# A spectral and gated-FFN kernel: new order and cut of the loads and of the first matmuls

## The chip, the core and the metric

The kernel runs on one core of one Trainium2 chip. The core has five engines that run beside each other: TensorE (PE, with its weight loads shown as PEld), VectorE (DVE), ScalarE (ACT), GpSimd (POOL) and SyncE (SP). [...] Matmuls write to PSUM; everything else lives in SBUF, and transfers from and to the device's memory (HBM) are issued by SP, ACT or POOL and carried by 16 DMA engines. The metric is the device time of one execution in microseconds. The page and the views quoted here come from one profiled execution.

## The reference

The input `x` has 2048 rows of 640 values. What is computed:

```python
xn = layernorm(x)                                  # over the 640 values of a row
X  = rfft2(xn) * (w_r + 1j * w_i)                  # over rows and columns, weights 2048 x 321
s  = irfft2(X, s=(2048, 640)).astype(bfloat16)
g  = silu((gelu(xn @ w_gate) * (xn @ w_up)) @ w_down)   # 640 -> 1536 -> 640
return x + s * g
```

All inputs are bf16. `B_x` is not used.

## The kernel before

**Tiling.** The 2048 rows are taken as 16 slabs of 128 rows (`n1` from 0 to 15; slab `n1` holds the rows n1, n1 + 16, and so on), which all live in the tile X. Four slabs make a group `g` of 512 rows. The FFN's inner width of 1536 is 12 tiles `t` of 128. Wg and Wu hold the gate and up weights as 5 row blocks (`c`, 128 rows each of the 640) by 1536 columns; Wd holds the down weights.

**Stages.** The two transforms are matrix products with cosine and sine tables that the kernel makes itself on POOL, DVE and ACT (Tinv, Tfwd, FT, FI, MG). The forward part works slab by slab (`slab_S1`, `slab_D`), goes through a scratch tensor ZDR in HBM, is read back as the tile B, multiplied by the weights W1 and W2 in eleven bursts (`s2_step`, tiles px, xs, pu), goes through a second scratch tensor UDR, and is transformed back (`slab_S1i`, `slab_Di`, `group_*`, `finish`). The FFN goes group by group: first the 12 tiles of gate and up products, then the down products, which for groups 1 and 2 are made with fewer multiplications from sums (`product`, `u_sum`, `w_sum`).

**The order of the work.** It is written out by hand. The list `back` holds the FFN's pieces in the order of PE, and `plan[s]` holds what is issued right after piece `s`; `put(s, ...)` adds to it. Every engine gets its instructions in that order and never changes it. The second stage starts at piece `sb`.

**The opening.** SP loads slab 0 (`load_x(0, 1)`) and slab 1, then up weights and the next slabs in turn; ACT loads the gate weights of tiles 0 to 5, two tiles at a time (`load_w(0, t, t + 2, nc.scalar)`). Each load of two tiles reads rows of 256 columns, 512 bytes. A load takes one of eight semaphores in turn, and so waits until the eighth load before it has landed. DVE makes the statistics of a slab in two halves (`bn_half`, line 189) and joins them (`bn_join`, line 195); the reciprocal root comes from ACT for slab 0 (`root_act`, line 214, which then also loads the table for Gelu) and from POOL for the others (`root`: `ve` on DVE, line 205, then a power on POOL, line 207). `norm_parts` normalises a slab in two parts, columns 0 to 383 and 384 to 639 (line 218). `slab_Tparts` transposes the slab on PE against the identity (line 994, tile pt) and copies the parts to the transposed tile xnT, in XG, the first on DVE and the second on ACT (line 995). While PE has nothing to do it runs fillers on a tile of ones (`warm_pe`, line 588, tile GEN): 21 at the start and 2 after the first transposes.

The order on DVE at the start is: statistics of slab 0, first half of slab 1, second half of slab 1, its join, its `ve`, and then the norm of slab 0:

```python
1136    warm_pe(21)
1137    bn_half(1, 1)
1138    bn_join(1)
1139    root(1, 1)
1140    norm_parts(0)
1141    slab_Tparts(0)
1142    warm_pe(2)
```

**The first pieces.** `ffn_piece(g, t, k, c0, c1_)` makes one tile `t` of gate (k = 0) or up (k = 1) for the columns c0 to c1_ of xnT: five matmuls, one for each row block, into a half or a quarter of a PSUM bank (psg or psu, two buffers each), and then the eviction: Gelu on ACT for the gate (line 837, tile ge), the product with ge on DVE for the up (line 839, tile UT). Group 0 starts with tiles 0 and 1 for slab 0 alone (128 columns), then for slab 1, then tiles 2 to 7 for slabs 0 and 1 (256 columns), then tiles 0 to 7 for slabs 2 and 3. These are 18 gate and 18 up pieces, each with an eviction of its own. From tile 8 on the pieces have all 512 columns.

Of the kernel before, what the change touches and what calls it, by code (L numbers as in the profile page):

```python
# [76 lines left out]
def build(nc, env):  # L77
    consts, big, wts, work, psA, psB = (env[k] for k in ("consts", "big", "wts", "work", "psA", "psB"))
    ZDR, UDR, X, Wg, Wu, Wd, W1, W2 = (env[k] for k in ("ZDR", "UDR", "X", "Wg", "Wu", "Wd", "W1", "W2"))
    xv, outv, wgv, wuv = (env[k] for k in ("xv", "outv", "wgv", "wuv"))  # L80
    A_w_r, A_w_i, B_w_down = (env[k] for k in ("A_w_r", "A_w_i", "B_w_down"))

    def load_x(n0, n, eng=nc.sync):
        eng.dma_start(out=X[:, n0:n0 + n, :], in_=xv[:, n0:n0 + n, :])

    def load_w(k, t0, t1, eng=nc.sync):
        f0, f1 = t0 * P, t1 * P
        eng.dma_start(out=(Wg, Wu)[k][:, :, f0:f1], in_=(wgv, wuv)[k][:, :, f0:f1])
# [12 lines left out]
    load_gu(6, 8)  # L101
    load_x(4, 4)
    load_gu(8, 12)
    load_x(8, 4)
    nc.sync.dma_start(out=Wd, in_=B_w_down.rearrange("(t p) d -> p t d", p=P))
    load_x(12, 4)

    spw = [(WT, src.rearrange("(k1 r) l -> k1 r l", k1=NS)) for WT, src in ((W1, A_w_r), (W2, A_w_i))]

# [63 lines left out]
    def c1(name, dt=FP32):  # L173
        return consts.tile([P, 1], dt, name=name)
# [11 lines left out]
    def bn_half(n1, k):  # L186
        if k == 0:
            st_n[n1] = work.tile([P, 2, nc.vector.BN_STATS_DIM], FP32, tag="st", bufs=3, name="st")
        nc.vector.bn_stats(out=st_n[n1][:, k, :], in_=X[:, n1, 320 * k:320 * k + 320])  # L189

    def bn_join(n1):
        g = n1 // 4
        if g not in mva:
            mva[g] = work.tile([P, 4, nc.vector.BN_AGGR_DIM], FP32, tag="mva", bufs=2, name=f"mva{g}")
        nc.vector.bn_aggr(out=mva[g][:, n1 % 4, :], in_=st_n[n1])

    def stats(n1):
        for k in range(2):
            bn_half(n1, k)
        bn_join(n1)  # L200

    def root(n0, n):
        m = mva[n0 // 4][:, n0 % 4:n0 % 4 + n, :]
        ve = work.tile([P, 4], FP32, tag="ve", name="ve")[:, 0:n]
        nc.vector.tensor_scalar(out=ve, in0=m[:, :, 1], scalar1=1e-5, scalar2=None, op0=ALU.add)  # L205
        r = work.tile([P, 4], FP32, tag="rst", bufs=4, name="rst")[:, 0:n]
        nc.gpsimd.tensor_tensor(out=r, in0=ve, in1=mhalf[:, 0:n], op=ALU.pow)  # L207
        rall[n0] = r
        for k in range(n):
            rstd[n0 + k] = r[:, k:k + 1]  # L210

    def root_act(n1):
        rstd[n1] = c1("rst0")
        nc.scalar.activation(out=rstd[n1], in_=mva[n1 // 4][:, n1 % 4, 1:2], func=ACT.Abs_reciprocal_sqrt, bias=eps)
        nc.scalar.activation(out=warm, in_=negpi, func=ACT.Gelu_apprx_tanh)

    def norm(n1, c0=0, c1_=D):
# [10 lines left out]
    eps = c1("eps")  # L228
    nc.vector.memset(eps, 1e-5)
# [95 lines left out]

    fwd_consts()
    vt_iota(0)
    stats(0)
    bn_half(1, 0)
    root_act(0)  # L330

# [252 lines left out]
    def warm_pe(n):  # L584
        if not warm_bank:
            warm_bank.append(bank(0))
        for _ in range(n):
            nc.tensor.matmul(warm_bank[0][:, 0:256], lhsT=ones[:, 0:P], rhs=ones, start=True, stop=True)
# [230 lines left out]
    def bank(k):  # L819
        return psA.tile([P, 512], FP32, tag="gu"[k], name="ps" + "gu"[k])  # L820
# [5 lines left out]
    def ffn_piece(g, t, k, c0, c1_):  # L826
        for j in range(c0 // P, c1_ // P):
            assert ("T", 4 * g + j) in done
        ps = bank(k)[:, c0:c1_]
        WT = (Wg, Wu)[k]  # L830
        for c in range(5):
            nc.tensor.matmul(ps, lhsT=WT[:, c, t * P:(t + 1) * P], rhs=xnT[g][:, c, c0:c1_],  # L832
                             start=(c == 0), stop=(c == 4))
# [7 lines left out]
    def ffn_part(g, t, h):  # L841
        for k in range(2):
            ffn_piece(g, t, k, h * 256, h * 256 + 256)

    def ffn_half(g, t, k):
        ffn_piece(g, t, k, 0, 512)
# [8 lines left out]
    def flush():  # L855
        now = put_off[:]
        del put_off[:]
        for f in now:
            f()
# [109 lines left out]
            if t == NT - 1:  # L969
                gated(g, j, k, ph)  # L970

    def ffn_slab(j, tk):
        for t, k in tk:
            ffn_piece(0, t, k, j * P, j * P + P)

    GG, UU = ((0, 0), (1, 0)), ((0, 1), (1, 1))

    def run(*items):
        for it in items:
            it[0](*it[1:])  # L980

    PARTS = ((0, 3), (3, 5))

    def norm_parts(n1):
        for a, b in PARTS:
            norm(n1, a * P, b * P)

    def slab_Tparts(n1):
        if n1 == 0:
            xnT[0] = slot(0, 5, 512)  # L990
        for (a, b), ev in zip(PARTS, (nc.vector.tensor_copy, nc.scalar.copy)):
            pt = psB.tile([P, 5, P], BF16, tag="b")
            for c in range(a, b):
                nc.tensor.transpose(out=pt[:, c, :], in_=X[:, n1, c * P:(c + 1) * P], identity=ident)  # L994
# [5 lines left out]
    back = [(run, (ffn_slab, 0, GG), (norm_parts, 1), (slab_Tparts, 1), (vt_iota, 1), (ffn_slab, 0, UU),  # L1000
             (inv_consts, 0), (inv_consts, 1)),
            (run, (ffn_slab, 1, GG + UU), (stats, 2), (root, 2, 1))]
    for h in range(2):
        for t in range(0 if h else 2, NP):
            back.append((ffn_part, 0, t, h))
        if h == 0:
            back[-1] = (run, (ffn_piece, 0, NP - 1, 0, 0, 256), (slab_Tparts, 3), (ffn_piece, 0, NP - 1, 1, 0, 256))
    for g in range(4):
        for t in range(NP if g == 0 else 0, NT):
            for k in range(2):  # L1010
# [10 lines left out]
    def put(s, *item):  # L1021
        plan[s].append(item)

    put(1, inv_rest)
    put(2, norm, 2)
    put(3, bn_half, 3, 0)
    put(4, bn_half, 3, 1)
    put(4, bn_join, 3)
    put(4, root, 3, 1)
    put(4, slab_T, 2, 1)  # L1030
    put(5, norm, 3)
    for g in range(5):
        put(3 + g, ft_v, g)
        put(8 + g, ft_v, 5 + g)
# [110 lines left out]

# [35 lines left out]
```

## Time and profile before

| | us |
|---|---|
| Median of 3 runs | 193.76 (193.47 to 193.83) |
| Profiled execution, its own time | 193.65 |
| Span in the profile, first to last instruction | 191.9 |
| PE busy | 186.1 (97%) |
| DVE busy | 150.9 (79%) |
| ACT busy | 131.9 (69%) |
| POOL busy | 53.9 (28%) |

The page gives the busy time of each engine, the chain of work that ended last, and groups of equal instructions. The chain is followed back from the last instruction: at each step to what released it, or to the instruction before it on its engine. The timeline lists instructions in order of time: start, duration, engine, line, operation, what it writes and reads, and in brackets the idle time of its engine just before and what ended it. A row that stands for several instructions has their count (x5). "SPq" and "ACTq" are the queues from which loads are issued. Matmul durations include the pipeline's length, so that they overlap; the distance between starts says what each costs.

### The profile page before, as it was taken

Reading aid. Unit: us, or ns where it says so; the run is one execution under the profiler, and the core shown is the slowest. Engines: PE = TensorE matmul, PEld = TensorE weight load, DVE = VectorE, ACT = ScalarE, POOL = GpSimd, SP = SyncE. Lnnn points to the kernel's source line nnn. Section 1 sums busy time; section 2 is a strip of 40 time slices with the busy share of each in tenths; the row PEclk is TensorE's granted clock in tenths of the full one; section 3 lists DMA queues with packets and bytes.
Section 4 is the critical chain, followed back from the end, with each engine's and each line's share of the span. In section 5 each row is a group of like instructions: output and inputs, shape, how many; then the busy total and the mean of one; then the engine's idle time right before and its main releaser. Section 6 shows DMA issues by size and latency. Waiting matters only on the chain.

```text
span 191.9 us, 4068 instructions
## 1 busy us (share of the span) xinstructions
PE 186.1 (97%) x1453; PEld 115.6 (60%) x1469; DVE 150.9 (79%) x364; ACT 131.9 (69%) x241; POOL 53.9 (28%) x91
## 2 busy tenths in 40 slices
PE   7999999999999999999999999999999999999993
PEld 5788854677655665566543334347775555556772
DVE  6787889899799889846978677685445898888973
ACT  4658557957878778536697878634989776876622
POOL 4458768999040200000000000002030134150400
PEclk9999999999999999999999999999999999999999
DMA  6999999948889994249996444149900084778842
GB/s 164 300 329 360 370 332 170 172 99 318 178 165 191 211 300 120 78 111 230 223 108 123 106 103 103 42 107 273 266 5 0 0 117 111 152 153 213 121 174 62
DMA packets 39700, 32.43 MB, mean 169 GB/s; under 512 B 12928, under 2 KB 37760, under 8 KB 39552
## 3 DMA queue, kind: packets, MB, share of 16 engines
q1 hardware_dynamic: 35888, 27.91, 58.6%
q0 software_dynamic: 1824, 3.28, 9.4%
q10 hardware_dynamic: 1968, 0.98, 1.9%
q8 instruction: 11, 0.18, 0.4%
q14 instruction: 9, 0.07, 0.1%
HBM read 19.03 MB, written 7.88 MB: 140 GB/s over the span
## 4 chain that ended last, share of the span: by engine, by line
PE 95%; DMA 2%; DVE 1%; issue 1%; SPq 0%; ACT 0%
PE psu L832 27%; PE psg L832 27%; PE psg L967 7%; PE psg L933 7%; PE psu L967 6%; PE psu L933 5%; PE pu L657 2%; PE pd L762 2%; PE pv L735 2%; PE pz L555 2%; PE pd L573 2%; PE px L628 2%; DMA X<-in_A_x_dram 2%; PE pt L994 1%; PE pd L575 1%
## 5 line engine op out<-in xcount | busy, mean ns | idle before, releaser
L832 PE MATMUL psu<-XG,Wu 128*128 128x512 bf16 (+2 forms) x284 | 60.4, 342 | 0.5 <-issue 0.3
L832 PE MATMUL psg<-XG,Wg 128*128 128x512 bf16 (+2 forms) x280 | 60.1, 341 | 0.6
L839 DVE TENSOR_TENSOR UT<-psu,ge 128x512 bf16<-128x512 f32 (+2 forms) x58 | 34.4, 594 | 13.6 <-PE psu L832 8.1
L837 ACT ACTIVATE ge<-psg 128x512 bf16<-128x512 f32 (+2 forms) x58 | 30.3, 523 | 21.3 <-PE psg L832 20.6
L832 PEld LDWEIGHTS <-Wu 128*128 128x128 bf16 x290 | 25.9, 98 | 20.9 <-issue 3.4
L832 PEld LDWEIGHTS <-Wg 128*128 128x128 bf16 x290 | 26.5, 98 | 18.8 <-issue 0.2
L967 PEld LDWEIGHTS <-UT 128*128 128x128 bf16 x204 | 19.1, 98 | 6.9
L813 POOL DMA_DIRECT2D VY<-in_A_x_dram x12 | 10.6, 964 | 26.2 <-ACT W L737 10.5
L713 POOL COPY vr<-VY 128x128 bf16<-128x128 bf16 x2 | 0.6, 291 | 60.2 <-DMA VY<-UDR 60.2
L644 DVE TENSOR_TENSOR RZ<-xs,W 128x960 bf16<-128x960 bf16 (+2 forms) x22 | 13.3, 647 | 4.4 <-ACT xs L640 4.4
L967 PE MATMUL psg<-Wd,UT 128*128 128x320 bf16 (+1 forms) x108 | 15.7, 290 | 0.0
L578 ACT CAST RZ<-pd 128x660 bf16<-128x660 f32 x16 | 11.3, 706 | 5.2 <-PE pd L575 5.2
L189 DVE BATCH_NORM_STATS2 st<-X 128x6 f32<-128x320 bf16 x32 | 14.0, 476 | 0.6 <-DMA X<-in_A_x_dram 0.4
L933 PEld LDWEIGHTS <-UT 128*128 128x128 bf16 x120 | 11.4, 98 | 4.8 <-issue 0.4
L967 PE MATMUL psu<-Wd,UT 128*128 128x320 bf16 (+1 forms) x96 | 13.9, 293 | 0.0
L737 ACT CAST W<-pv 128x640 bf16<-128x640 f32 x16 | 11.1, 691 | 3.1 <-PE pv L735 3.1
L763 ACT ACTIVATE W<-pd 128x640 bf16<-128x640 f32 x16 | 11.3, 706 | 1.5 <-PE pd L762 1.5
L557 ACT CAST GEN<-pz 128x640 bf16<-128x640 f32 x16 | 11.2, 698 | 1.2 <-PE pz L555 1.2
L672 ACT CAST RX<-pu 128x480 bf16<-128x480 f32 (+3 forms) x22 | 10.8, 489 | 1.1 <-DVE RX L672 0.3
L640 ACT CAST xs<-px 128x960 bf16<-128x960 f32 (+2 forms) x11 | 10.3, 933 | 0.0
L207 POOL TENSOR_TENSOR rst<-ve,mhalf 128x1 f32<-128x1 f32 (+1 forms) x6 | 5.5, 913 | 11.5 <-DVE ve L205 11.5
L933 PE MATMUL psg<-X,UT 128*128 128x320 bf16 x48 | 7.8, 300 | 0.0
(202 smaller groups left out, 302.1 us busy)
## 6 DMA issues: line engine op xcount, KB each, us to landing
ZDR<-RZ SPq DMA_DIRECT2D x16, 160.5 KB, 4.1
UDR<-RX SPq DMA_DIRECT2D x10, 240.8 KB, 3.1
B<-ZDR SPq DMA_DIRECT2D x8, 240.8 KB, 5.2
W<-UDR SPq DMA_DIRECT2D x2, 963.0 KB, 9.1
X<-in_A_x_dram SPq DMA_DIRECT2D x3, 640.0 KB, 10.3
Wd<-in_B_w_down_dram SPq DMA_DIRECT2D x1, 1920.0 KB, 14.6
VY<-in_A_x_dram POOLq DMA_DIRECT2D x12, 160.0 KB, 4.3
out_dram<-VY SPq DMA_DIRECT2D x12, 160.0 KB, 2.8
```

The lines of the kernel that those rows point to most:

```text
L189: nc.vector.bn_stats(out=st_n[n1][:, k, :], in_=X[:, n1, 320 * k:320 * k + 320])
L557: nc.scalar.copy(out=Zt[n1], in_=pz)
L578: nc.scalar.copy(out=zd.rearrange("p c (q e) -> p c q e", e=10), in_=pd[:, :, 0:330].rearrange("p c (e q) -> p c q e", q=33))
L644: nc.vector.tensor_tensor(out=pp[-1], in0=xs, in1=WT[:, :, h0:h0 + n, l0:l0 + w], op=ALU.mult)
L672: copy(out=out, in_=src)
L737: nc.scalar.copy(out=vs, in_=pv)
L763: nc.scalar.activation(out=parts(eobuf, i, 5)[:, :, n1 - DG[i][0], :], in_=pd, func=ACT.Copy, scale=(2.0 if n1 // 4 in BY_SILU else 1.0) / ...
L832: nc.tensor.matmul(ps, lhsT=WT[:, c, t * P:(t + 1) * P], rhs=xnT[g][:, c, c0:c1_], start=(c == 0), stop=(c == 4))
L837: nc.scalar.activation(out=ges[t], in_=ps, func=ACT.Gelu_apprx_tanh)
L839: nc.vector.tensor_tensor(out=UT[:, t, c0:c1_], in0=ps, in1=ges[t], op=ALU.mult)
L933: nc.tensor.matmul(ps, lhsT=lhs[:, t, :], rhs=rhs[:, t, :], start=(t == 0 and i in (0, 1, 3)), stop=(t == 5), skip_group_check=i in (2, 4, ...
L967: nc.tensor.matmul(ph, lhsT=UT[:, t, j * P:(j + 1) * P], rhs=Wd[:, t, c0:c1_], start=(t == 0), stop=(t == NT - 1))
```

## The change

Six things change.

1. **Gate and up weights of tiles 0 to 3 come in row parts.** `load_w` takes a range of row blocks; a part holds the row blocks 0 to 2 or 3 to 4 of four tiles, with rows of 512 columns (1024 bytes). ACT loads the two gate parts. SP loads the two up parts. Tiles 4 to 7 come as one load for each of gate and up, also with 512 columns.
2. **Two small POOL copies hold loads back.** One writes a single column of Wu from the first half of slab 0's statistics; the up parts overwrite that column, so SP waits for it. The other writes a single column of slab 2's place in X from normalised slab 0; the load of slab 2 overwrites it, so SP waits for it, and with it all later loads, which now stand behind it.
3. **Slab 0's norm and transposes come before the second half of slab 1's statistics.** Slab 1's root is made on ACT as well, and the Gelu table is loaded after it. Both copies of the transposes of slabs 0 and 1 go to DVE. The fillers are 18 and 4 instead of 21 and 2.
4. **The first pieces have another shape.** `ffn_quad` makes tiles 0 to 3 for one slab in one bank: 20 matmuls of 128 columns, the row blocks 0 to 2 of all four tiles first, then 3 and 4, and one eviction. `ffn_multi` makes two tiles for 256 columns in one bank: 10 matmuls, one eviction. The order is: quads for slab 0, quads for slab 1, tiles 4 to 7 for slabs 0 and 1, tiles 0 to 7 for slabs 2 and 3.
5. **Statistics, roots, norms and transposes of slabs 2 and 3 and the constants for the inverse tables** (`inv_consts`, `inv_rest`) are issued at other pieces.
6. **The second stage and all that follows it starts two pieces earlier** (`sb` is 65 instead of 67).

```diff
-    def load_w(k, t0, t1, eng=nc.sync):
+    def load_w(k, t0, t1, eng=nc.sync, c0=0, c1_=5):
         f0, f1 = t0 * P, t1 * P
-        eng.dma_start(out=(Wg, Wu)[k][:, :, f0:f1], in_=(wgv, wuv)[k][:, :, f0:f1])
+        eng.dma_start(out=(Wg, Wu)[k][:, c0:c1_, f0:f1], in_=(wgv, wuv)[k][:, c0:c1_, f0:f1])
...
+    PARTS = ((0, 3), (3, 5))
     load_x(0, 1)
     load_x(1, 1)
-    load_w(1, 0, 2)
-    load_w(1, 2, 4)
-    load_x(2, 1)
-    load_w(1, 4, 6)
-    load_x(3, 1)
-    load_gu(6, 8)
...
-    for t in (0, 2, 4):
-        load_w(0, t, t + 2, nc.scalar)
+    for part in PARTS:
+        load_w(0, 0, 4, nc.scalar, *part)
...
-    stats(0)
+    bn_half(0, 0)
+    nc.gpsimd.tensor_copy(out=Wu[:, 0, 0:1], in_=st_n[0][:, 0, 0:1])
+    for part in PARTS:
+        load_w(1, 0, 4, nc.sync, *part)
+    bn_half(0, 1)
+    bn_join(0)
     bn_half(1, 0)
     root_act(0)
...
+    def ffn_quad(k, j, *part):
+        assert ("T", j) in done
+        if part[0] == 0:
+            cur["m"] = bank(k)
+        ps = cur["m"].rearrange("p (t w) -> p t w", w=P)
+        WT = (Wg, Wu)[k]
+        for a, b in [PARTS[i] for i in part]:
+            for i in range(4):
+                for c in range(a, b):
+                    nc.tensor.matmul(ps[:, i, :], lhsT=WT[:, c, i * P:(i + 1) * P],
+                                     rhs=xnT[0][:, c, j * P:(j + 1) * P], start=(i + c == 0), stop=(c == 4),
+                                     skip_group_check=True)
+        if part[-1] == 1:
+            multi_out(k, 0, ps, j * P, j * P + P)
+
+    def ffn_multi(k, t0, n, c0, c1_, half=None):
...
+        for i in range(n) if half is None else range(half * n // 2, (half + 1) * n // 2):
+            for c in range(5):
+                nc.tensor.matmul(ps[:, i, :], lhsT=WT[:, c, (t0 + i) * P:(t0 + i + 1) * P], rhs=xnT[0][:, c, c0:c1_],
+                                 start=(c == 0), stop=(c == 4))
+        if half != 0:
+            multi_out(k, t0, ps, c0, c1_)
...
-        for (a, b), ev in zip(PARTS, (nc.vector.tensor_copy, nc.scalar.copy)):
+        for (a, b), ev in zip(PARTS, (nc.vector.tensor_copy, nc.scalar.copy if n1 > 1 else nc.vector.tensor_copy)):
...
+    back = [(run, (ffn_quad, 0, 0, 0, 1), (vt_iota, 1)),
+            (run, (ffn_quad, 1, 0, 0), (slab_Tparts, 1), (ffn_quad, 1, 0, 1)),
+            (ffn_quad, 0, 1, 0, 1),
+            (ffn_quad, 1, 1, 0, 1)]
+    for h, k, t0 in ((0, 0, 4), (0, 0, 6), (0, 1, 4), (0, 1, 6)) + tuple((1, k, t) for t in (0, 2, 4, 6) for k in range(2)):
+        back.append((ffn_multi, k, t0, 2, 256 * h, 256 * h + 256))
+    back[6] = (run, (ffn_multi, 1, 4, 2, 0, 256, 0), (slab_T, 2, 1), (ffn_multi, 1, 4, 2, 0, 256, 1))
+    back[7] = (run, (ffn_multi, 1, 6, 2, 0, 256, 0), (slab_Tparts, 3), (ffn_multi, 1, 6, 2, 0, 256, 1))
...
-    put(1, inv_rest)
-    put(2, norm, 2)
-    put(3, bn_half, 3, 0)
-    put(4, bn_half, 3, 1)
-    put(4, bn_join, 3)
-    put(4, root, 3, 1)
-    put(4, slab_T, 2, 1)
-    put(5, norm, 3)
+    put(1, stats, 2)
+    put(1, root, 2, 1)
+    put(2, bn_half, 3, 0)
+    put(2, bn_half, 3, 1)
+    put(3, norm, 2)
+    put(3, bn_join, 3)
+    put(3, root, 3, 1)
+    put(3, inv_consts, 0)
+    put(3, inv_consts, 1)
+    put(4, inv_rest)
+    put(5, norm_parts, 3)
...
-    sb = 67
+    sb = 65
...
-    warm_pe(21)
+    warm_pe(18)
+    norm_parts(0)
+    nc.gpsimd.tensor_copy(out=X[:, 2, 0:1], in_=X[:, 0, 0:1])
+    load_x(2, 1)
+    load_w(0, 4, 8)
+    load_x(3, 1)
+    load_w(1, 4, 8)
...
+    slab_Tparts(0)
+    warm_pe(4)
     bn_half(1, 1)
     bn_join(1)
-    root(1, 1)
-    norm_parts(0)
-    slab_Tparts(0)
-    warm_pe(2)
+    root_act(1)
+    gelu_table()
+    norm_parts(1)
```

More of the change, by code (lines that the diff above doesn't have):

```diff
@@ L839, in ffn_piece, with multi_out @@
             nc.vector.tensor_tensor(out=UT[:, t, c0:c1_], in0=ps, in1=ges[t], op=ALU.mult)
-    def ffn_part(g, t, h):
-        for k in range(2):
-            ffn_piece(g, t, k, h * 256, h * 256 + 256)
+    def ffn_quad(k, j, *part):
[13 more added lines that the diff above has]
+    def ffn_multi(k, t0, n, c0, c1_, half=None):
+        w = c1_ - c0
+        for j in range(c0 // P, c1_ // P):
+            assert ("T", j) in done
+        if half in (None, 0):
+            cur["m"] = bank(k)[:, 0:n * w].rearrange("p (t w) -> p t w", w=w)
+        ps = cur["m"]
+        WT = (Wg, Wu)[k]
+        for i in range(n) if half is None else range(half * n // 2, (half + 1) * n // 2):
[4 more added lines that the diff above has]
+            multi_out(k, t0, ps, c0, c1_)
+    def multi_out(k, t0, ps, c0, c1_):
+        n, w = 512 // (c1_ - c0), c1_ - c0
+        flush()
+        if k == 0:
+            ge = work.tile([P, 512], BF16, tag="ge", bufs=3, name="ge")[:, 0:n * w].rearrange("p (t w) -> p t w", w=w)
+            ges[t0, c0] = ge
+            nc.scalar.activation(out=ge, in_=ps, func=ACT.Gelu_apprx_tanh)
+        else:
+            nc.vector.tensor_tensor(out=UT[:, t0:t0 + n, c0:c1_], in0=ps, in1=ges[t0, c0], op=ALU.mult)
     def ffn_half(g, t, k):
```

26 lines of the change are left out of this document (7 added, 19 removed).

## The prediction

> **What bounds the kernel now.** I read the page first (shares of the span, the chain that ended last), then the chain over 0 to 12 us, the timeline there, and the DMA rate by stretches.
>
> ```profile
> span 191.9 us, 4068 instructions
> PE 186.1 (97%) x1453; PEld 115.6 (60%) x1469; DVE 150.9 (79%) x364; ACT 131.9 (69%) x241; POOL 53.9 (28%) x91
> ...
> PE 95%; DMA 2%; DVE 1%; issue 1%; SPq 0%; ACT 0%
> ```
>
> PE is the chain for 95% of the span; what another engine saves counts only where PE waits for it. That is at the start, which the chain shows in order of time (start, us, what):
>
> ```profile
> 1.17 3.19 DMA X<-in_A_x_dram
> 4.38 0.90 DVE st L189 x2
> 5.30 0.22 DVE mva L195
> 5.55 0.15 DVE ve L205
> 5.70 0.30 DVE X L218
> 6.05 0.54 PE pt L994 x5
> 6.59 0.22 PE psg L588 x2
> 6.84 0.76 PE psg L832 x10
> ...
> 8.44 0.56 PE psg L832 x10
> ...
> 10.65 0.55 PE psg L832 x5
> ```
>
> Useful matmuls begin at 6.84 us. Before that the chain runs through the statistics of slab 1 (both halves, aggregate, `ve`), although the matmuls wait for slab 0. From 6.84 on the pieces follow each other: ten of 128 columns in 0.56 us (56 ns each), five of 256 in 0.545 (109 ns each). The timeline shows what slab 0 alone needed, and when slabs 2 and 3 came:
>
> ```profile
> 1.18 4.55 PE L588 MATMUL psg<-GEN 128*128 128x256 bf16 x21 [1.18 <-DVE eps L229]
> 2.75 1.00 POOL L258 IOTA GEN<- 128x1024 int32 x1 [1.05 <-DVE GEN L257]
> ...
> 4.29 0.29 ACT L214 ACTIVATE rst<-mva,eps 128x1 f32<-128x1 f32 x1 [2.08 <-DVE mva L195]
> ...
> 9.87 0.88 DVE L189 BATCH_NORM_STATS2 st<-X 128x6 f32<-128x320 bf16 x2
> ...
> 12.56 0.48 DVE L189 BATCH_NORM_STATS2 st<-X 128x6 f32<-128x320 bf16 x1
> ```
>
> Slab 0's root is ready at 4.58, yet its norm starts at 5.62, a microsecond later. Last the DMA (PE, PEld, DVE, ACT, POOL busy, clock, DMA share, GB/s):
>
> ```profile
> 8.00:10.00 2.00, 2.00 (x34) 1.94 (x32) 1.65 (x12) 0.84 (x3) 1.56 (x4) 1.00 1.14 302
> 10.00:12.00 2.00, 2.00 (x20) 1.79 (x19) 1.60 (x6) 1.15 (x3) 0.72 (x2) 1.00 1.14 306
> ...
> 16.00:20.00 4.00, 4.00 (x41) 3.52 (x38) 3.12 (x9) 3.29 (x10) 3.92 (x4) 1.00 1.08 368
> ```
>
> The engines are full in all three. Weights in tiles of two (rows of 512 B) move at 302 to 306 GB/s; later loads with rows of 1 KB and more at 368.
>
> **The change, part by part.** *Norm of slab 0 ahead of slab 1.* The second half of slab 1's statistics, its aggregate and `ve` leave the path; the first half stays. It starts when slab 1 lands (4.38) and lets the next DVE instruction in about 0.42 us later (two take 0.89). So the norm starts at 4.80 instead of 5.62: -0.82. Transposes follow 0.43 later as now: 5.23. If the wider weight rows slow slab 1's landing, this moves with it; I bound that by ±0.3 and take 0.
>
> *Copies and fillers.* 18 fillers end at 1.18 + 18 x 0.217 = 5.08, so there is no wait for them. The evictions of slab 0 both go to DVE, 0.36 plus at most 0.36 (row L995); the second is only wanted by the thirteenth matmul, 0.67 us in. Four fillers instead of two sit between transposes and matmuls. They begin 0.38 after the transposes begin, 5.61; at 109 ns they end at 6.05, at 217 ns at 6.48. I take 6.05, since two in 0.38 us here fit the faster pace (0.27 for one alone plus 0.11). Start of useful work: 6.84 to 6.05, -0.79; the other end is -0.36.
>
> *Quads and pairs.* The same columns: 80 matmuls of 128 and 120 of 256 for 40 and 140: 80 x 0.0556 + 120 x 0.109 = 17.53 against 17.48, +0.05. Evictions become 8 pairs instead of 18: ACT 8 x 0.58 = 4.6 for 6.4 us, DVE 8 x 0.69 = 5.5 for 6.5 (4 x 0.29 + 13 x 0.41). That is worth nothing, since they wait for PE (20.6 us of ACT's idle time); it only spares DVE.
>
> *Held-back ups.* SP now waits, before the first up part, for a POOL copy that needs the first statistics (done 3.61) and stands on POOL behind an iota until 3.75. No row has that copy: 0.13 (an iota of one column) to 0.29 (a copy of 128); I take 0.2. SP issues at about 4.0 instead of 1.64, and everything behind it on SP waits too. It is wanted at 6.05 + 20 x 0.0556 = 7.16. Issue to landing was 2.4 us for 160 KB (shortest X row) and 3.1 us for 320 KB late in the kernel (RX, page part 6); this is 384 KB beside the rest of the gates. Earliest 6.4, latest 4.0 + 5.4 = 9.4 by the shortest of today's ups, queued behind others. Nearest is the 320 KB row, plus 64 KB at 350 GB/s: 7.3. (350 is my estimate between 303 and 368, nearer the second, since all these rows now have 1 KB or more.) So +0.15 (0 to 2.2). The second part is two thirds as large, lands 0.75 later and is wanted 0.67 later, after the transposes of slab 1 (0.28): hidden.
>
> *Held-back later loads.* The second POOL copy waits for slab 0's norm (5.2), SP issues slab 2 at about 5.5. Behind it stand gates 4 to 8, slab 3, ups 4 to 8, and all later loads; on POOL the second iota and the lists wait, which ACT first needs after 10 us. Today's queue is itself held: slab 3 is issued at 4.38, the next gates at 7.07, the next ups at 8.85, each when an earlier load lands. Data in order at 350 GB/s: ups complete about 8.0, slab 2 8.5, gates 10.4, slab 3 10.9, ups 12.7. Wanted: gates at 10.9, ups at 13.1. Covered by half a microsecond each, +0; at 303 GB/s the ups come at 13.6, +0.5. The whole stream to the last slab has the same bytes, in 14 loads on SP for 15 and 2 on ACT for 3 (0.4 to 0.6 us of queue each), so later stages see it no later.
>
> *Slab 1's norm and the tables.* ACT now does two roots before the Gelu table (1.28 us): slab 1's root at 7.0, table until 8.6, first Gelu at 8.8 instead of 7.36. Cover: its bank is wanted again at 10.9. Slab 1's norm starts at 7.35, its transposes can start at 7.8; PE comes at 7.16 + 0.15 + 0.67 = 7.98: +0. Gelu releases the first product on DVE at 9.4, so slab 2's statistics run from 10.0, slab 3's from 11.3, slab 3's norm ends near 14.9. PE wants it at 15.0, and its copy on DVE, behind a product, ends 0.1 after PE asks: +0.1 (0 to 0.5).
>
> *Inverse constants, second stage two steps earlier.* Five DVE instructions (0.29) and six on POOL (1.7 with gaps) move some 3 us later on an idle POOL; ACT needs them at 17.5: +0. The first burst of the second stage (SP's first loads at 82.94, shortest landing 3.6; PE asks at 89.60) is asked for two products earlier, about 88.0: +0, with -0.2 to +0.5 for its DVE and ACT work among the products.
>
> Sum: -0.79 + 0.05 + 0.15 + 0.10 = -0.49. The profiled execution took 193.65 (span 191.9 and 1.75 around it): 193.16. The median shown is 193.76, 0.11 above it; I say 193.2.
>
> [...]
>
> **The rivals.** *The held ups come late (slower).* Place: the first up part at PE's first quad of ups. If it takes 4.3 us from issue, the shortest that any weight load shows today (4.3/6.4/10.3 us), it lands at 8.3, 1.15 after PE asks: 193.65 - 0.79 + 0.05 + 1.15 + 0.1 = 194.2. For it: all weight loads so far are that slow. Against: they stood in a full queue. It decides from a landing at 7.8.
>
> *The clock rises later (no change).* The fillers run at 217 ns now, matmuls after them at 109. If the rise comes after slab 0's transposes, the four fillers add 0.43: 193.6. [...]
>
> *The rate stays at 303 (no change).* The first ups come at 7.5 (+0.35 for 0.15), ups 4 to 8 at 13.6 (+0.5): 193.86. For it: 302 and 306 in the rows; against: 368.
>
> *More than forecast.* Without ups in the queue slab 1 lands 0.3 earlier and no load is late: 193.65 - 1.09 + 0.05 + 0.1 = 192.7.
>
> **How the numbers follow.** Forecast 0.50 (own range 192.9 to 193.5), late ups 0.25, later clock 0.09, rate 0.08, more gain 0.08. A measurement of this kernel can tell about 0.2%, 0.39 us. Faster: 0.45 of the forecast's 0.50 and the last case, 0.53; same: 0.05 + 0.09 + 0.08 = 0.22; slower 0.25. The range runs from between the larger gain and the forecast to just past the late ups, 192.8 to 194.3; the latest landing (9.4) lies outside.
>
> **What would show it.** Right: norm of slab 0 at 4.8, transposes at 5.2, first useful matmul at 6.05; PE idle at the first ups under 0.3 us; a dense chain from there, g = 1 starting 0.5 earlier. Wrong: PE idle over 0.7 us before a matmul on Wu or Wg; fillers after the transposes at 217 ns; a wait of PE for X of slab 3; or PE idle near 88 to 92 us, where the second stage now meets the products.

## The result: 0.7% slower, and the profile after

The changed kernel takes 195.01 us (median of 6 runs, 194.25 to 195.15) where the kernel before takes 193.7 in the same comparison: a ratio of 1.0066, with a 95% interval of 1.0054 to 1.0078. The forecast was 193.2, with 194.3 as the upper end of the range. It was wrong in sign and outside the range.

The page of the changed kernel (the span, the busy times, the shares of the chain) says at once that the chain is no longer PE's alone:

```profile
span 192.6 us, 4077 instructions
...
PE 186.5 (97%) x1472; PEld 116.1 (60%) x1488; DVE 151.9 (79%) x358; ACT 130.0 (68%) x230; POOL 53.3 (28%) x92
...
PE 87%; DVE 4%; DMA 4%; issue 2%; ACT 0%; SPq 0%; POOL 0%; DVEq 0%
```

PE was 95% of the chain before and is 87% now; DVE has 4% and DMA 4%. The chain's start, in order of time (start, us, what), names the way that they came in:

```profile
4.69 0.39 DVE X L211
5.08 0.05 issue
5.13 0.24 POOL X L1168
5.37 0.02 issue
5.39 0.34 SPq L84
5.73 0.04 issue
5.77 5.95 DMA Wg<-in_B_w_gate_dram
11.72 0.05 issue
11.77 2.36 PE psg L864 x20
```

Slab 0's norm lets the second POOL copy go (line 1168), that lets SP issue slab 2, behind it the gates of tiles 4 to 7 are issued at 5.77, they land at 11.72, and PE waits for them until 11.77. So the chain of this execution runs through the wait that the change adds on SP; what that wait is worth in time only the experiments can tell. PE's own timeline gives the sizes:

```profile
5.63 0.81 PE L586 MATMUL psg<-GEN 128*128 128x256 bf16 x4
6.27 1.28 PE L848 MATMUL psg<-XG,Wg 128*128 128x128 bf16 x20
7.65 0.83 PE L848 MATMUL psu<-XG,Wu 128*128 128x128 bf16 x12
...
11.77 2.36 PE L864 MATMUL psg<-XG,Wg 128*128 128x256 bf16 x20 [0.28 <-DMA Wg<-in_B_w_gate_dram]
14.09 0.72 PE L864 MATMUL psu<-XG,Wu 128*128 128x256 bf16 x5
```

The sizes are taken from start to start, since the brackets count from the modelled end of the instruction before. Useful work starts at 6.27 for 6.84. Twenty matmuls of 128 columns take 1.11 us, so the first ups should follow at 7.38 and come at 7.65: 0.27. The two quads of slab 1 should end at 11.33, and the next piece starts at 11.77: 0.44. Its 20 matmuls of 256 columns take 2.18, so the ups of tiles 4 to 7 were due at 13.95 and come at 14.09: 0.14. At tile 8 (the first pieces of 512 columns) the kernel stands at 25.58 against 25.24. The balance closes: -0.57 + 0.05 (more matmuls) + 0.27 + 0.44 + 0.14 = +0.33 for +0.34.

A second loss lies at 30 us. The timeline of POOL, DVE, ACT and PE there:

```profile
22.80 1.49 POOL L372 TENSOR_TENSOR GEN<-GEN 128x660 f32<-128x660 f32 x1
...
23.13 1.73 DVE L337 TENSOR_SCALAR GEN<-GEN,andm,orm 128x1024 int32<-128x1024 int32 x1
...
26.52 0.17 DVE L196 TENSOR_SCALAR ve<-mva 128x4 f32<-128x4 f32 x1
...
26.77 1.53 POOL L198 TENSOR_TENSOR rst<-ve,mhalf 128x4 f32<-128x4 f32 x1 [2.47 <-DVE ve L196]
...
28.57 0.20 POOL L454 TENSOR_TENSOR nmr<-nm,rst 128x4 f32<-128x4 f32 x1
...
28.80 0.92 ACT L459 ACTIVATE X<-X,nmr,rst 128x640 bf16<-128x640 bf16 x1 [3.52 <-DMA W<-in_A_w_r_dram]
...
29.63 0.58 ACT L835 ACTIVATE ge<-psg 128x512 bf16<-128x512 f32 x1
...
30.25 1.24 PE L830 MATMUL psg<-XG,Wg 128*128 128x512 bf16 x5 [0.20 <-ACT ge L835]
```

And the same work in the kernel before:

```profile
21.21 1.49 POOL L374 TENSOR_TENSOR GEN<-GEN 128x660 f32<-128x660 f32 x1
...
22.81 0.81 DVE L339 TENSOR_SCALAR GEN<-GEN,andm,orm 128x1024 int32<-128x1024 int32 x1
...
26.81 0.92 ACT L461 ACTIVATE X<-X,nmr,rst 128x640 bf16<-128x640 bf16 x1 [1.54 <-POOL nmr L456]
...
27.64 0.58 ACT L837 ACTIVATE ge<-psg 128x512 bf16<-128x512 f32 x1
```

POOL's table work runs 1.6 us later, because `inv_consts` and `inv_rest` were moved behind. Its 1.49 us operation now falls on DVE's mask (the operation with `andm` and `orm`), which takes 1.73 us for 0.81. The variance of slabs 4 to 7, their root and ACT's norm follow (28.80 for 26.81; its bracket names a load, but POOL's `nmr`, which the norm reads, ends at 28.77, and in the kernel before the bracket names `nmr`). Gelu waits behind the norm on ACT, and PE waits for Gelu's bank: a due start at 29.90, a start at 30.25, 0.35. From 34 to 86 us PE's stages stand 0.78 us behind. Then the earlier start of the second stage changes the order (its matmuls come 0.8 to 1.8 us earlier than before, products 1.2 to 1.6 later), and the span ends 0.7 longer.

The last part is in no view of the instructions. The time around the span was 1.75 us in the profiled execution of before and is 2.16 here (194.76 less 192.6). Over the runs its median is 1.78 before and 2.12 after. So the profiled execution lost 0.34 in the opening, 0.35 at 30 us and 0.41 outside the span: 1.1 us, from 193.65 to 194.76.

### The profile page after: what moved, and what is told of

The parts are those of the page before. It is cut to its first block, busy times and chain, and to the rows that moved or that the text cites. A ratio compares the mean times of both kernels' runs of the same rounds, so it can differ in the third digit from the quotient of the medians.

```text
span 192.6 us, 4077 instructions
## 1 busy us (share of the span) xinstructions
PE 186.5 (97%) x1472; PEld 116.1 (60%) x1488; DVE 151.9 (79%) x358; ACT 130.0 (68%) x230; POOL 53.3 (28%) x92
## 4 chain that ended last, share of the span: by engine, by line
PE 87%; DVE 4%; DMA 4%; issue 2%; ACT 0%; SPq 0%; POOL 0%; DVEq 0%
PE psu L830 21%; PE psg L830 21%; PE psg L1001 7%; PE psg L967 7%; PE psu L1001 6%; PE psu L967 5%; DMA Wg<-in_B_w_gate_dram 3%; PE pu L655 2%; PE pv L733 2%; PE psg L864 2%; PE psu L864 2%; PE pd L760 2%; PE pz L553 2%; PE pd L571 2%; DVE st L180 2%; PE px L626 2%
## 5 line engine op out<-in xcount | busy, mean ns | idle before, releaser
L830 PE MATMUL psu<-XG,Wu 128*128 128x512 bf16 x194 | 49.0, 379 | 0.5 <-issue 0.3
L830 PE MATMUL psg<-XG,Wg 128*128 128x512 bf16 x190 | 48.7, 379 | 0.7 <-ACT ge L835 0.2
L837 DVE TENSOR_TENSOR UT<-psu,ge 128x512 bf16<-128x512 f32 x40 | 27.4, 687 | 10.7 <-PE psu L830 6.8
L835 ACT ACTIVATE ge<-psg 128x512 bf16<-128x512 f32 x40 | 23.9, 596 | 15.5 <-PE psg L830 14.6
L830 PEld LDWEIGHTS <-Wu 128*128 128x128 bf16 x200 | 18.0, 98 | 20.3 <-issue 3.4
L830 PEld LDWEIGHTS <-Wg 128*128 128x128 bf16 x200 | 18.6, 98 | 18.4 <-issue 0.5
L735 ACT CAST W<-pv 128x640 bf16<-128x640 f32 x16 | 11.1, 700 | 3.1 <-PE pv L733 3.1
L555 ACT CAST GEN<-pz 128x640 bf16<-128x640 f32 x16 | 11.1, 696 | 1.2 <-PE pz L553 1.2
L670 ACT CAST RX<-pu 128x480 bf16<-128x480 f32 (+3 forms) x22 | 10.8, 489 | 1.4 <-DVE RX L674 0.7
L875 ACT ACTIVATE ge<-psg 128x512 bf16<-128x512 f32 x8 | 4.8, 595 | 6.5 <-PE psg L864 5.1
L198 POOL TENSOR_TENSOR rst<-ve,mhalf 128x4 f32<-128x4 f32 (+1 forms) x5 | 5.4, 1071 | 11.0 <-DVE ve L196 8.5
```

The lines of the kernel that those rows point to most:

```text
L555: nc.scalar.copy(out=Zt[n1], in_=pz)
L670: copy(out=out, in_=src)
L735: nc.scalar.copy(out=vs, in_=pv)
```

## The experiments

Each ratio is to the kernel before on the same chip. Landing times are those at which the last of the 16 DMA engines reports in the trace, in us from the span's start.

### The two copies and the constants, one at a time

Without the first copy (it held the ups):

```diff
-    nc.gpsimd.tensor_copy(out=Wu[:, 0, 0:1], in_=st_n[0][:, 0, 0:1])
```

> Edit: the changed kernel without its first POOL copy, so that SP issues the two up parts right behind slab 1, near 1.7 us instead of 4.0. The second hold stays. Theory S (the holds leave the DMA engines empty, 178 GB/s from 5 to 6 us and 226 from 8 to 9, and the late loads stop PE): the ups land by 6.5, PE's 0.27 us wait at the first ups goes, gates 4 to 8 land about 0.5 earlier than 11.7, so 0.4 to 0.7 us less than the changed kernel, near 194.4. Rival G (the ups take the gates' bandwidth, which is what a hold is for): the first quad of gates starts late, after 6.7 us instead of 6.27, and the time is that of the changed kernel or longer, 195.0 or more.

Measured: 194.5 us, ratio 1.0046 (1.0029 to 1.0064), 0.2% better than with it, a difference that the two intervals don't separate. PE no longer waits at the ups. It waits 0.51 us inside the first quad: with the ups issued beside it the second gate part lands at 7.03 (5.77 in the changed kernel), where PE asks at 6.56. The gates of tiles 4 to 7 still come 0.27 late. So the first copy does what it is meant for, protect the gates; it moves the wait more than it makes one. The wait near 30 us stays (0.30), with a mask of 1.67 us.

Without the second copy (it held slab 2 and all behind it):

```diff
-    nc.gpsimd.tensor_copy(out=X[:, 2, 0:1], in_=X[:, 0, 0:1])
```

> Edit: the changed kernel without its second POOL copy, so that slab 2 and all later loads are issued right behind the ups, near 4.9 us instead of 5.4. Theory S: the dip at 8 to 9 us fills, gates 4 to 8 land at about 11.2, PE's waits of 0.44 and 0.14 us go, 0.4 to 0.6 us less than the changed kernel, near 194.4. Rival B (the opening is bound by bytes in order and not by the issue): gates 4 to 8 land at 11.7 as before and the time stays at 195.0.

Measured: 195.44 us, ratio 1.0079 (1.0054 to 1.0104): no better. That was a miss for the theory that the hold makes the wait, and the rival had 11.7 for a landing that came at 13.34. The profiled execution was the longest of its five (194.62 to 196.63 us), and its PE timeline shows what it waited for:

```profile
13.39 1.81 PE L864 MATMUL psg<-XG,Wg 128*128 128x256 bf16 x15 [1.84 <-DMA Wg<-in_B_w_gate_dram]
```

The first engine had done its share of these gates at 9.73, the last at 13.34. Nothing in this kernel's issues explains 3.6 us between them; the three loads issued before it had 0.9 at most. What held the last engine stays open, and whether the other four executions had such a lag is not shown. The mask took 1.84 us here, and PE waited 0.47 near 32 us.

Both copies left out:

> Edit: the changed kernel without both POOL copies. Theory S: the DMA engines are full from 3 us, all loads of the opening come at least 1 us earlier, every wait of PE on them (0.27, 0.44, 0.14) goes: 0.8 us less than the changed kernel, near 194.2, with the wait behind ACT near 30 us left. Rival G: the gates land late and PE starts later by as much as it gains, 195.0.

Measured: 194.15 us, ratio 1.0024 (1.0012 to 1.0037), better than the changed kernel by 0.4%. The DMA rate by stretches (the last column; the one before is the DMA share) shows what the copies do to the stream. With them, in the changed kernel:

```profile
5.00:6.00 1.00, 1.00 (x8) 0.80 (x8) 0.66 (x4) 0.00 (x0) 0.23 (x1) 1.00 0.78 178
7.00:8.00 1.00, 0.91 (x17) 0.76 (x15) 0.64 (x3) 0.98 (x2) 0.04 (x1) 1.00 0.95 286
8.00:9.00 1.00, 1.00 (x22) 1.00 (x20) 0.32 (x2) 0.99 (x3) 1.00 (x2) 1.00 0.82 226
```

Without the copies:

```profile
5.00:6.00 1.00, 1.00 (x9) 0.82 (x9) 0.66 (x3) 0.00 (x0) 0.00 (x0) 1.00 1.07 365
...
7.00:8.00 1.00, 0.96 (x17) 0.79 (x15) 0.65 (x3) 0.98 (x2) 0.12 (x1) 1.00 1.10 361
8.00:9.00 1.00, 1.00 (x21) 1.00 (x19) 0.07 (x1) 0.99 (x3) 1.00 (x2) 1.00 1.10 347
```

Each hold leaves a hole in the stream, 178 and 226 GB/s where 347 to 365 are to be had. By 9 us 1.96 MB have moved with the copies (a mean of 218 GB/s) and 2.37 MB without (263), which is 1.1 us of the stream. The gates of tiles 4 to 7 landed at 10.29 instead of 11.72: 0.64 of this is the first engine (9.55 for 10.19), the rest the lag of the last one (0.74 for 1.54). No wait for a load is left behind 8 us.

But that is not where the time was gained. The quads now waited for the second gate part, the clock rose at 6.71, and at tile 8 this execution stood at 25.54, where the changed kernel stood at 25.58. It gained at 30 us: POOL's operation came 0.87 earlier, the mask met only its last 0.33 us, and PE did not wait there.

```profile
21.93 1.49 POOL L371 TENSOR_TENSOR GEN<-GEN 128x660 f32<-128x660 f32 x1
...
23.09 0.88 DVE L336 TENSOR_SCALAR GEN<-GEN,andm,orm 128x1024 int32<-128x1024 int32 x1
```

So leaving out both copies also removes the second loss, and this ratio alone can't price the copies.

The constants alone, issued early again, both copies kept:

```diff
+    put(0, inv_consts, 0)
+    put(0, inv_consts, 1)
+    put(1, inv_rest)
     put(1, stats, 2)
...
-    put(3, inv_consts, 0)
-    put(3, inv_consts, 1)
-    put(4, inv_rest)
```

> Edit: the changed kernel with the inverse constants made early again (the five on DVE behind the first piece, the six on POOL ahead of the statistics of slab 2). Theory C (POOL's late chain is the second loss: its tensor_tensor at 22.8 us meets DVE's mask, which takes 1.73 instead of 0.81 us, the statistics, root and norm of slabs 4 to 7 follow 1.5 to 2 us late on DVE, POOL and ACT, and ACT's Gelu behind the norm stops PE for 0.35 us at 29.9): POOL runs its tables about 1.4 us earlier, the mask takes 0.81 again, no wait of PE near 30 us, 0.35 us less than the changed kernel, near 194.7. Rival: the mask is slow for another reason and PE waits as it did, 195.0.

Measured: 194.14 us, ratio 1.0031 (1.0015 to 1.0046), better than the changed kernel by 0.35%, where the trace had shown 0.35 us or 0.18%. Of the rest 0.29 us stood in the opening of the profiled execution (25.29 at tile 8 for 25.58), where the order of work is the same: the gates of tiles 4 to 7 landed at 11.23 and PE did not wait for them, but the ups landed at 7.82 and PE waited 0.6 us there. These landings differ between executions. The mask is short again and PE has no wait near 30 us:

```profile
21.06 1.49 POOL L372 TENSOR_TENSOR GEN<-GEN 128x660 f32<-128x660 f32 x1
...
22.84 0.76 DVE L337 TENSOR_SCALAR GEN<-GEN,andm,orm 128x1024 int32<-128x1024 int32 x1
```

### What is left when both are mended

Both copies left out and the constants early:

> Both small POOL copies are gone, and the constants for the inverse tables are issued at pieces 0 and 1, ahead of slab 2's statistics; all else is as in the changed kernel. Theory S (the loss is what the two copies hold back, plus the collision of POOL's tables with DVE's mask near 30 us): the two repairs add up, 1.0066 less 0.0042 less 0.0035 gives a ratio of 0.999, 193.4 us against 193.6; no wait of PE over 0.3 us before 32 us. Rival R (the new cut of the loads and the matmuls costs something itself, or the time outside the span does): the ratio stays at 1.002 or more, 194.0 us, although PE has no waits.

Measured: 194.23 us, ratio 1.0031 (1.0016 to 1.0047). The two repairs don't add up, and the rival held: the new cut costs something of its own. The four kernels side by side, each with its ratio and the mask's time in its profile:

| | constants late | constants early |
|---|---|---|
| both copies | 1.0066, 1.73 us | 1.0031, 0.76 us |
| no copies | 1.0024, 0.88 us | 1.0031, 0.76 us |

The time is long only where the mask is long. With the constants early the copies make no difference in it. What is left, 0.3%, lies in different places: by the medians, with the copies 0.2 us in the span and 0.3 around it, without them some 0.5 and 0.1. Without the copies it is not a cost without a wait, as the rival had it:

```profile
5.92 0.83 PE L847 MATMUL psg<-XG,Wg 128*128 128x128 bf16 x12
7.61 0.62 PE L847 MATMUL psg<-XG,Wg 128*128 128x128 bf16 x8 [0.86 <-DMA Wg<-in_B_w_gate_dram]
```

The first part of the gates was used up at 6.59 and the second landed at 7.56: 1.02 us between due and start. All that the early start had won went there. A second wait, 0.3 us that ends at 16.99, is for the copies of slab 3's transposes.

Two edits of the same kernel, one number each: the second stage back at 67, and two fillers for four.

```diff
-    sb = 65
+    sb = 67
```

> As the run with both copies gone and the constants early, but the second stage starts at piece 67 as before the change, not 65. Theory P (the start of the second stage is worth nothing): the same time as that run within 0.15%. Rival Q (two pieces earlier costs in the middle of the kernel, where the span of the changed kernel was up to 1.8 us behind at 95 us and 0.7 at the end): 0.3 us faster or more, 193.1.

Measured: 194.61 us, ratio 1.0056 (1.0041 to 1.0071), slower than with 65 by 0.25%. Neither theory had that sign. Its profiled execution was already 0.25 behind at tile 8, long before the edit does anything, so only some 0.15 of the 0.4 us by which its span is longer can be the second stage's. With four executions the difference may be chance.

```diff
-    warm_pe(4)
+    warm_pe(2)
```

> As the run with both copies gone and the constants early, but with 2 fillers for 4 after the first transposes. Theory F (fillers are lost time where the clock has not risen): the first useful matmul comes 0.2 to 0.4 earlier and the time falls by 0.1 to 0.3 us. Rival G (PE then waits for the copy of the transposed slab, or the clock rises later by as much): no difference beyond 0.15%.

Measured: 194.2 us, ratio 1.0033 (1.0018 to 1.0047): no difference. PE waited 0.3 for the copy of slab 0 instead, and then 0.65 for the second gate part. The rival held: with a wait for data behind them, two fillers more or less made no difference (1.0031 and 1.0033).

### Part 3 and part 6 alone, on the kernel before

The reorder alone (slab 0's norm and transposes first, 18 fillers), with the old loads and pieces:

```diff
-    warm_pe(21)
+    warm_pe(18)
+    norm_parts(0)
+    slab_Tparts(0)
     bn_half(1, 1)
     bn_join(1)
     root(1, 1)
-    norm_parts(0)
-    slab_Tparts(0)
     warm_pe(2)
```

> The kernel before, with nothing changed but the place of slab 0's norm and transposes, now ahead of the second half of slab 1's statistics, and 18 fillers for 21. Theory 1 (the reorder alone can't pay, since slab 0's work of tiles 0 and 1 lasts 1.1 us and slab 1's norm now comes 0.9 us later): first useful matmul at about 6.0 for 6.84, then PE waits 1 us or more for the transposes of slab 1; 193.6 to 194.2 us. Rival 2 (the reorder is where a gain comes from, and the rest of the change spoils it): 193.0 us, with no wait over 0.3 us.

Measured: 194.22 us, ratio 1.0032 (1.002 to 1.0045), as the first theory had it, at the upper end of its range:

```profile
5.97 0.95 PE L832 MATMUL psg<-XG,Wg 128*128 128x128 bf16 x10
7.89 0.54 PE L994 MATMUL pt<-ident,X 128*128 128x128 bf16 x5 [0.96 <-DVE X L218]
```

Useful work starts at 5.97, 0.87 earlier, and PE then waits 0.96 for slab 1's norm. This is what the quads of the change are for: they give PE 2.2 us of work on slab 0 alone.

The second stage alone:

```diff
-    sb = 67
+    sb = 65
```

> The kernel before with one part of the change alone: the second stage starts at piece 65, not 67. Theory P (forecast: worth nothing): ratio 1.000, within 0.001. Rival Q (the earlier start helps, as the two runs with 65 and 67 pieces, 194.23 and 194.61, suggest): ratio 0.998 to 0.999, 193.2 to 193.4 us. If it is above 1.001 the earlier start is part of the loss.

Measured: 193.91 us, ratio 1.0008 (0.9993 to 1.0023). No difference that shows; the gain that the pair with 65 and 67 had suggested is not there.

### Is it the supply of weights?

The quads ask for weights faster than the queues bring them in any of these traces (up to 418 GB/s over a microsecond of the changed kernel's opening): a quad of 20 matmuls reads 20 blocks of 32 KB in 1.11 us, 590 GB/s. The pieces of before use each weight for slab 0 and again for slab 1: tiles 0 and 1 (655 KB) last 2.24 us, 290 GB/s, where their loads brought about 300. Two kernels ask for it, both made from the one with the copies out and the constants early. In the first SP issues all loads of the opening, in order of use:

```diff
     for part in PARTS:
-        load_w(0, 0, 4, nc.scalar, *part)
+        load_w(0, 0, 4, nc.sync, *part)
```

> As the run with both copies gone and the constants early, with one thing moved: the two gate parts are issued by SP behind slabs 0 and 1 and ahead of the up parts, not by ACT. Theory D (the opening's loads come in the wrong order: two queues share the engines, so the second gate part lands at 7.6 beside the ups where PE asks for it at 6.8, and PE waits 0.9 to 1.0 us): at the 350 GB/s of these rows one queue in order of use lands slabs 0 and 1 by 3.2, the gates by 5.6, the ups by 7.0 and 7.8, all before PE asks; the wait goes, 0.8 to 1.0 us of span, 193.3 us for 194.2, ratio 0.998 to 0.999. Rival E (one queue brings less at the start than two, or the time of the opening goes elsewhere, to the clock or to the transposes of slab 3): 193.9 or more.

Measured: 194.28 us, ratio 1.0029 (1.0018 to 1.004). The wait at the second gate part is gone (it landed at 6.72), and the next one is at the ups, which land at 7.80 where they are due at 7.17:

```profile
6.06 1.32 PE L847 MATMUL psg<-XG,Wg 128*128 128x128 bf16 x20
7.84 0.84 PE L847 MATMUL psu<-XG,Wu 128*128 128x128 bf16 x12 [0.46 <-DMA Wu<-in_B_w_up_dram]
```

The order alone doesn't cure it. My 7.0 for this landing was near the first engine's 6.69; the last came 1.1 us after. The time around the span is 1.78 in the profiled execution and 1.81 in the median, nearly as in the kernel before; three of the twelve executions have 2.3 to 2.4.

In the second the quads of ups read the gate weights, which are there already, and every load stays:

```diff
-        WT = (Wg, Wu)[k]
+        WT = Wg
```

> As the run with all loads of the opening on SP's queue, but the two quads of ups read the gate weights instead of the up weights (so the up half of tiles 0 to 3 is computed from other data); every load stays. In this kernel no piece needs an up weight of tiles 0 to 3 before 9 us. Theory D (the quads ask for weights at 20 x 32 KB in 1.11 us, 590 GB/s, and the queues bring 350, so PE waits 0.3 to 1.0 us at the second half of the first weights or at the first ups in every arrangement): PE has no wait for a DMA before 11 us, and the time falls by 0.4 to 0.7 us, to 193.7 or less, a ratio of 1.000 or below. Rival K (what is won there is lost behind it, because the transposes of slab 1 or the banks then stop PE, or because the clock rises in that time anyway): within 0.2 us of the run it is made from.

Measured: 193.61 us, ratio 0.9997 (0.9982 to 1.0012), 0.32% or 0.6 us better than the kernel it is made from:

```profile
5.79 1.39 PE L847 MATMUL psg<-XG,Wg 128*128 128x128 bf16 x20
7.01 0.83 PE L847 MATMUL psu<-XG,Wg 128*128 128x128 bf16 x12
```

No wait is left between the quads, and the time falls as the theory of supply said. This run prices the opening without the copies: with weights that keep up, all the rest of the new opening makes the time of before, and with the real ones the quads cost 0.6 us. For the kernel with the copies no such run was made. It also shows that the forecast gain would not have come even then. Its profiled execution started useful work 1.05 earlier than before (with the clock risen at 4.28, the earliest of all) and was 0.28 ahead at tile 8; of the difference 0.32 is the wait for slab 3's copies and some 0.26 are waits for the gates and ups of tiles 4 to 7.

That wait was tried by itself, on the kernel with all loads on SP:

```diff
-    back[7] = (run, (ffn_multi, 1, 6, 2, 0, 256, 0), (slab_Tparts, 3), (ffn_multi, 1, 6, 2, 0, 256, 1))
+    back[7] = (run, (slab_Tparts, 3), (ffn_multi, 1, 6, 2, 0, 256))
```

> As the run with all loads of the opening on SP's queue, and the transposes of slab 3 issued before the whole last piece of slabs 0 and 1, not in the middle of it. Theory T (PE's 0.3 us at 16.8 us is a wait for the copies of slab 3's transposes, which stand on DVE behind a product, and twice the work on PE covers it): a further 0.3 us, 193.0. Rival N (slab 3's norm comes no earlier, so PE waits for it instead at the transposes): no difference from the run on SP's queue beyond 0.1%.

Measured: 193.89 us, ratio 1.0022 (1.0002 to 1.0041), not to be told from 1.0029. The transposes then stood on PE 0.28 us longer, with the second part of slab 3's norm still to come: the rival's wait.

### An early start without quads

Last, two kernels that keep the small pieces of before and cover slab 1's norm in another way: up tile 0 of slab 0 goes ahead of slab 1's transposes, and slab 1's statistics and root ahead of slab 0's copies.

```diff
-    warm_pe(21)
+    warm_pe(18)
+    norm_parts(0)
     bn_half(1, 1)
     bn_join(1)
     root(1, 1)
-    norm_parts(0)
     slab_Tparts(0)
...
-    back = [(run, (ffn_slab, 0, GG), (norm_parts, 1), (slab_Tparts, 1), (vt_iota, 1), (ffn_slab, 0, UU),
+    back = [(run, (ffn_slab, 0, GG), (norm_parts, 1), (ffn_slab, 0, UU[:1]), (slab_Tparts, 1), (vt_iota, 1), (ffn_slab, 0, UU[1:]),
```

> The kernel before with its own loads and small pieces, in another order of work: slab 0's norm, then the second half of slab 1's statistics, join and root, then slab 0's transposes (18 fillers for 21), and up tile 0 of slab 0 ahead of slab 1's transposes, so that slab 1's norm is covered. Theory D (the reorder is worth its 0.5 us where the weights keep up; with these loads up tiles 0 and 1 land at 7.1 and are wanted at 6.8, and later loads have no slack): first useful matmul at 6.2 to 6.3, waits of 0.3 to 0.5 us for DMA after it, net 0.0 to 0.2 us faster, 193.4 to 193.6. Rival L (an earlier start only buys slower matmuls, since the clock rises between 4.5 and 7.1 us whatever stands on PE): no gain even where no wait shows.

Measured: 193.7 us, ratio 1.0002 (0.9986 to 1.0019). Useful work starts at 6.41 (slab 0's copy came later than I had it), and then up tile 0, due at 6.97, starts at 7.97: its load landed at 7.92 in this profiled execution, 7.05 in that of before. The 0.4 us won and more went there, with loads that are the same. But this was the longest of the twelve executions (194.56 us); where the median one lost the start's gain is not shown.

```diff
-    load_w(1, 0, 2)
-    load_w(1, 2, 4)
+    load_gu(0, 2)
+    load_gu(2, 4)
     load_x(2, 1)
+    load_w(0, 4, 8)
     load_w(1, 4, 6)
+    load_w(1, 6, 8)
     load_x(3, 1)
-    load_gu(6, 8)
...
-    for t in (0, 2, 4):
-        load_w(0, t, t + 2, nc.scalar)
```

> As the run before this with the loads of the opening on SP alone, in order of use: slabs 0 and 1, gates and ups 0 and 1, gates and ups 2 and 3, slab 2, gates 4 to 7, ups 4 and 5, ups 6 and 7, slab 3. Demand by the weights is now about 300 GB/s from 6.2 us on, against 590 in the quads. Theory D: no DMA wait over 0.3 us before 14 us, first useful matmul at 6.2, 193.1 to 193.3, ratio 0.997 to 0.9985. Rival L: within 0.001 of the kernel before although no wait shows.

Measured: 195.34 us, ratio 1.0085 (1.0063 to 1.0107), a clear miss. Up to 11.4 us PE waited 0.25 at most and was 0.2 ahead, in spite of a clock that rose only at 6.37. Then tile 4's gate came 0.33 late, its up 0.57, and slab 3, which I had put last, so late that PE waited 0.6 for its norm at 17.0. By tile 8 it was 1.3 us behind. As I read it, an opening made faster only meets the end of the same stream earlier; the late place of slab 3 is not priced apart from that. Whether the clock takes part of an early start was not told apart (in 16 profiles it rises between 4.28 and 6.90 us, where the rival had 4.5 to 7.1); no version here is faster than the kernel before.

## Why the prediction was wrong, step by step

- *"Norm of slab 0 ahead of slab 1": right.* Norm at 4.69 for 4.80, transposes at 5.12 for 5.23.
- *"At 109 ns they end at 6.05": 0.22 off.* The four fillers ran from 5.63 to 6.27; two of them had 0.21 us, because the clock rose at 6.04 and not, as before, at 5.48. These are the times at which the granted clock's first record begins in the two traces; fillers start 0.21 us apart ahead of it and 0.11 behind it. The transposes were slow too (0.51 us to the fillers for 0.38), which took back the 0.11 of their earlier start. The rival on the clock was real at half its size. Over 16 profiles of these kernels the rise lies between 4.28 and 6.90 us, at 5.07 and 6.90 in two whose openings are the same. What sets that time no run here shows.
- *"Held-back ups +0.15": 0.27, and the landing of 7.3 was 7.51.* The right mechanism and nearly the right size, with some luck: the rival "the held ups come late" decides from 7.8, and with the same hold the ups landed at 7.82, 0.6 us late, in the run with the constants early.
- *"Held-back later loads ... Covered by half a microsecond each, +0": failed.* It measured 0.44 + 0.14 in the changed kernel. I let the data flow at 350 GB/s without a break and gave the gates 10.4. The rate was right where the queue was full (341 to 418 GB/s with rows of 1 KB or more; weights with 512 B rows came at 300 to 324 from 4 to 9 us in the last run, where SP alone issued them). But the two holds empty the queue for parts of a microsecond (178 GB/s from 5 to 6 us, 226 from 8 to 9), and a load's landing is that of its slowest engine: slab 2's load took from 8.03 to 9.91 from the first engine to the last. I had written down when SP issues, and not what the engines do between two issues. Without the copies the gates landed at 10.29, near my figure, and at 10.8 to 11.1 in the three further runs of that kind. As a price for the copies the 0.58 does not stand: with the constants early the ratio is 1.0031 with them and without.
- *"Quads and pairs ... +0.05": the cost on PE was right, the demand was not asked for; failed.* I checked one landing against one time, 7.3 against 7.16. The quads' need of 590 GB/s follows from the same numbers, 20 x 32 KB in 1.11 us. The quads wait by 0.2 to 1.0 us in all ten profiles with real weights, at the second gate part or at the ups; the smallest wait (0.21) is in a run where the clock rose at 6.71, after the quads had begun, and the first matmuls were slow. Without the copies the run with the gate weights in the ups prices it at 0.6 us.
- *"Inverse constants ... on an idle POOL: ACT needs them at 17.5: +0": failed.* POOL was idle, but the tables behind the constants moved too, into DVE's mask. I looked at the next user of the constants, not at what stands behind them on POOL and who runs beside it then. It is 0.35 us in the trace, and the run that mends it gains 0.35%, or 0.7 us. The wait near 30 us is in the three profiles with a long mask and in none of the others.
- *"Slab 3's copy +0.1 (0 to 0.5)": right, but hidden in the changed kernel* behind the waits for gates and ups; in the runs without the copies it shows, at 0.3.
- *"Second stage +0": right*, 1.0008 (0.9993 to 1.0023) alone.
- *"1.75 around it": taken as fixed, and it grew by 0.3 to 0.4.* It is 2.1 to 2.2 in every kernel with at least one copy, 1.9 to 2.0 without copies where ACT issues the gate parts, and 1.8 where SP issues all, as in the kernel before (where ACT issues three loads, too). What runs there is in no record; the cause stays open.

So what failed is the overlap: each moved load and each moved piece of POOL's work was held against one user and called covered. Two terms decide: the constants moved on an idle POOL (+0, and 0.7 us by the runs), and the quads (+0.05, and 0.6 us by the runs without the copies, because PE asks for weights faster than they come). The waits of the runs overlap, so they don't sum: whoever takes one away meets the next. With the copies kept, most of what is left is the time around the span, and its cause is not known.

## What to carry to other kernels

At the start of a kernel compare two curves, not single landings: the bytes that PE has asked for and the bytes that the queues can have brought. Here taking four tiles of weights for one slab, where the pieces of before take two tiles for two slabs in the same time, doubled the first curve (590 GB/s for 290), and the start moved ahead was paid back at the next load (waits of 0.2 to 1.0 us). The waits that held a queue back left holes in the stream (178 and 226 GB/s, for 347 to 365 without them) as well as delaying what they held. A repair that shortens the time need not have worked at the place it was made for: here leaving out the copies also moved POOL's work off the mask (0.88 us for 1.73). And when work is moved on an idle engine, follow all that stands behind it there to whom it will run beside: here it made that mask 1.73 us long for 0.81.

## What the runs showed of the hardware

- **DVE beside POOL.** The first of DVE's two masks over 1024 int32 takes 0.76 to 0.88 us in 13 of 16 profiles. In the three where most of POOL's tensor_tensor over 660 f32 (1.1 to 1.3 of its 1.49 us) runs beside it, it takes 1.67, 1.73 and 1.84; an overlap of 0.33 goes with 0.88. Why the mask is longer beside it no run here shows.
- **The engines of one load.** The 16 engines finish a load that lands in the first 10 us 0.4 to 1.3 us apart in the kernel before and 0.3 to 1.9 in the changed one, and the loads behind it keep the lag: 0.8 to 1.0 at every load that lands from 8 to 14 us before, 1.5 to 1.9 at the four from slab 2 to the ups of tiles 4 to 7 after; without the second copy it was 3.6 at one load. Landings differ between profiles of kernels with the same loads: the gates of tiles 4 to 7 came at 11.72 in the changed kernel and at 11.23 with the constants early.
- **Before the first instruction or after the last.** Some 0.3 to 0.4 us of the loss is seen only in the device time, largest where a copy holds a load (2.1 to 2.2 us around the span, for 1.8). The cause is open.
